# The last row tile's probabilities of pairs 5 to 16: 32x32 transposes in place by VectorE, blocks moved by ScalarE and GpSimd

## The chip, the core and the metric

The kernel runs on one core of a Trainium2 chip. The metric is the device time of one execution in microseconds (us), taken over several runs. Five engines work side by side: TensorE (PE in the profile; its weight loads are a row of their own, PEld), VectorE (DVE), ScalarE (ACT), GpSimd (POOL) and SyncE (SP), which issues all DMAs here. Each runs its own instructions strictly in the order in which the program lists them, and waits on semaphores for the others.

## The reference

Attention with a causal mask and a bias from a running sum, then two mixture layers on the result (shapes: 4 batches, 8 heads, 576 positions, head size 64):

```python
scores = scale * np.matmul(q, k.transpose(0, 1, 3, 2))
cum = np.cumsum(np.maximum(s, 0.0), axis=-1)
bias = -(cum[:, :, :, None] - cum[:, :, None, :])
scores = np.where(causal, -1000000000.0, scores + np.minimum(bias, 0.0))
attn = np.exp(scores - np.max(scores, axis=-1, keepdims=True))
attn = attn / (np.sum(attn, axis=-1, keepdims=True) + 1e-09)
x = np.matmul(attn, v)                                     # then (2304, 512)
x = np.maximum(np.maximum(x @ w1, x @ w2), x @ w3) @ w_out # d_ff 768
h = x @ w_in                                               # d_ff 2048
g = (a[0] + a[1]*h + a[2]*h**2 + a[3]*h**3) / (1.0 + abs(b[0])*abs(h) + abs(b[1])*h**2 + 1e-6)
out = g @ w_out2
```

## The kernel before

**Pairs.** The 32 heads go in 16 pairs (`pr` 0 to 15 in the code; pairs 1 to 16 in the title). The two heads of a pair (`y` 0 and 1) lie in the two halves of the partitions. For each pair the scores are made in five row tiles of queries, `i` 0 to 4: 64 rows, then four times 128. Causality cuts the keys, so tile `i` holds 64 + 128 `i` keys per head, and the last one, tile 4, is 128 queries by 576 keys.

**One pair, step by step.** `scores` makes the products on TensorE in four groups of two PSUM banks; VectorE adds the mask, takes the row minimum of the negated scores and writes the tile `P[i]` in SBUF (one buffer each); ScalarE takes the exponential in place and sums the rows; `norm` divides by the sum, on GpSimd or ScalarE. `flip` then turns each 128x128 block of `P` with keys on the free axis into one with keys on the partitions: a TensorE transpose against `ident` into a PSUM bank, and a copy of the bank (by ScalarE or VectorE) into the SBUF tile `PT`. There are six flip groups a pair, listed in `TBK`: tiles 2, 1, both heads of tile 4 apart, and both heads of tile 3 apart. 64-wide end blocks of both heads are flipped together ("lone" blocks, line 540; the others are line 545) and land in `PTC`. `values` multiplies the flipped probabilities by V on TensorE (line 597, two heads side by side in the array) into a group of 320 and one of 256 queries, and the result is split into a high and a low part, the tile `x` of the pair.

**What surrounds it.** Four pairs make one batch. The products of the first mixture layer for a batch (`experts`, line 187, 128x288) are issued among the attention steps of the next batch, 12 to a result; the last batch has its own stretch after the last pair. The second mixture layer (lines 187 and 944, 384 and 512 columns) fills the rest. Its weights and those of the first layer are loaded as raw words (`raww`), decoded by three VectorE steps (lines 639, 642, 644) and, for the second layer, written to DRAM (`w2_dram`, 36 "spills") and read back into `ws` tiles, once the SBUF of attention is given up.

**The order.** A planner (`Plan.issue`) sets the order on every engine when the program is built: each step has a rank, a cost written into the code for each engine that may take it, and what it reads and writes. A step that may run on several engines (`anyof`) goes where the cost, weighted by a price per engine, is least at that moment. A DMA's end is reckoned from a wire rate. On the chip only the order remains; the costs play no part.

Of the kernel before, what the change touches and what calls it, by code (L numbers as in the profile page):

```python
# [8 lines left out]
F32 = mybir.dt.float32  # L9
# [15 lines left out]
class Plan:  # L25
# [38 lines left out]
    def issue(self):  # L64
# [71 lines left out]
def kernel(  # L136
# [92 lines left out]
    PR = lambda pr: None if pr > 3 else {"dve": 1.0, "act": 1.0, "pool": 0.8}  # L229
# [37 lines left out]
    mask = at.tile([128, S + 128], F32, name="mask")  # L267
# [8 lines left out]
    P = [at.tile([128, 2 * (r0 + nr)], F32, name=f"P{i}") for i, (r0, nr) in enumerate(IT)]  # L276
# [73 lines left out]
    def consts():  # L350
        nc.gpsimd.memset(mask, 0.0)
        for at0, n, base in ((S, 128, 0), (0, 64, -64), (64, 64, 0)):
            nc.gpsimd.affine_select(
                out=mask[:, at0:at0 + n], in_=mask[:, at0:at0 + n], compare_op=ALU.is_ge,
                fill=-BIG / scale, base=base, pattern=[[-1, n]], channel_multiplier=1)

# [36 lines left out]
    plan.add({"pool": 1.2}, 0.1, lambda: pads(1), (), [("vh", 1, y) for y in range(2)], pre=e_dma)  # L393

# [46 lines left out]
    SB = [[(2, 0, 320, 0), (1, 0, 192, 320)], [(0, 0, 64, 0), (4, 0, 320, 64)], [(4, 320, S, 0)], [(3, 0, 448, 0)]]  # L441

    TBK = [((2, (0, 1)), ()), ((1, (0, 1)), (1, 2, 0)), ((4, (0,)), ()), ((4, (1,)), ()), ((3, (0,)), ()), ((3, (1,)), (3, 4))]
# [6 lines left out]
    def scores(pr, gs, rank):  # L450
# [3 lines left out]
        u = pr % 2  # L454
        Q, K, E = QK["q"][u], QK["k"][u], EXT[u]
        holds = {g: [Hold(), Hold()] for g in gs}
        sm = smalls[u]
        ops = [(Q[:, 0], K[:, 0]), (Q[:, 0], K[:, 1]), (Q[:, 1], K[:, 0]), (E[:, 1], E[:, 0])]

        def mms():  # L460
            for g in gs:
                for i, j0, j1, at0 in SB[g]:
                    r0, nr = IT[i]
                    b1, nb = 2 * i - j0 // 64, (j1 - j0) // 64
                    for x, (l, r) in enumerate(ops):
                        for y in range(2):
                            h = slice(64 * y, 64 * y + 64)
                            keys = r[h, j0:j1]
                            if y and i:
# [7 lines left out]
        for g, i, j0, j1, at0 in [(g, *x) for g in gs for x in SB[g]]:  # L477
# [4 lines left out]
            for y in range(2):  # L482
                m0 = S if i == 0 else j0 if y else S + 128 - W + j0
                m = smc(y, i)
                Pi = P[i][:, y * W:y * W + W]
                part = 3 if (i == 4 and j0 == 0) else 0
                ve(rank + 0.02, j1 - j0, lambda y=y, i=i, j0=j0, j1=j1, at0=at0, m=m, Pi=Pi, part=part, nr=nr, m0=m0, hold=hold:
                   nc.vector.tensor_tensor_reduce(  # L488
                       Pi[0:nr, j0:j1], hold[y].bank[0:nr, at0:at0 + j1 - j0], mask[0:nr, m0:m0 + j1 - j0], -scale,
                       sm[0:nr, 3, m:m + 1] if (i == 4 and j0 > 0) else 3.0e38, ALU.add, ALU.min, sm[0:nr, part, m:m + 1]),  # L490
                   [("sb", pr, g), ("s turn", g % 2), "const"] + ([("m3", pr, y)] if j0 > 0 else []),
                   [("P", y, i)] + ([("m3", pr, y)] if part else [("mn", pr, y, i)]), free=[hold[y]] if last else (),
                   cost=c_dve(j1 - j0))
                if j1 == W:
                    ac(rank + 0.04, 0, lambda Pi=Pi, W=W, m=m, nr=nr: nc.scalar.activation(  # L495
                        out=Pi[0:nr, 0:W], in_=Pi[0:nr, 0:W], func=ACTF.Exp,
# [9 lines left out]
    def norm(pr, tiles, rank):  # L506
# [10 lines left out]
        for i in tiles:  # L517
            for y in range(2):
                r0, nr = IT[i]
                t = P[i][0:nr, y * (r0 + nr):(y + 1) * (r0 + nr)]  # L520
                m = smc(y, i)
# [6 lines left out]

    def flip(pr, g, rank):
        hold = Hold()  # L530
        (i, ys), lone = TBK[g]
        n = 128 * i * len(ys)

        def tr():


            for x in ((), (), (1, 0), (1, 0, 2))[len(lone)]:
# [9 lines left out]
        def ev(e):  # L547
# [11 lines left out]
            if lone:  # L559
# [7 lines left out]
              [("tb", pr, g), ("t turn", t_turn(pr, g))], [("PT", g)], [hold], e_dma if pr == 0 else (), PR(pr))  # L567
# [14 lines left out]
    def values(pr, gis, rank):  # L582
# [8 lines left out]
        work = [[x for x in w if x[2] < x[3]] for w in work]  # L591

        def mms():
            for gi, b0, b1, hold in parts:
                for lone, j, q0, q1 in work[gi]:
                    for y in range(2):
                        nc.tensor.matmul(  # L597
                            hold.bank[64 * y:64 * y + 64, q0 - b0:q1 - b0], VH[u][:, j, y] if lone else V[u][y][:, j],
                            PTC[:, 64 * LONE[j]:64 * LONE[j] + 64] if lone else PTT[:, PH * y + SKEW * j + q0 - 64:PH * y + SKEW * j + q1 - 64],
# [3 lines left out]
        gs = [g for g in range(6) if (1 if g > 1 else 0) in gis]  # L603
        pe(rank, sum(0.01 + 4 * (q1 - q0) / 2400.0 for gi in gis for _, _, q0, q1 in work[gi]), mms,
# [415 lines left out]
```

## Time and profile before

| | |
|---|---|
| median of 3 runs | 889.09 us (888.07 to 890.43) |
| the profiled execution | 888.37 us |
| its span, first to last instruction | 886.6 us (1.8 us lie around it) |
| TensorE busy | 874.3 us, 99% of the span |
| VectorE, ScalarE, GpSimd busy | 663.2, 503.1, 341.0 us |
| granted TensorE clock, mean | 0.998 |

Busy times are sums of the instructions' spans. A matmul's span covers its way through the array, while the next one has already begun, so the busy share of TensorE does not tell how fast one follows another; the chain of work and the starts of instructions do.

### The profile page before, as it was taken

The numbers are of one execution on the slowest core, as the hardware profiler recorded it, in microseconds if no ns is written. First come the engines' busy times: TensorE is split into PE (matmuls) and PEld (weight loads), VectorE is DVE, ScalarE is ACT, GpSimd is POOL, SyncE is SP. The second block draws the span as 40 slices with busy tenths as digits, with TensorE's granted clock in tenths as the row PEclk, the third lists the DMA queues.
The fourth block names the chain that finished last, engine by engine and source line by source line (L and its number), as shares of the span: only waits on it lengthen the run. The fifth ranks groups of instructions, "written<-read, shape, count | busy, mean of one in ns | idle before, by whom it ended". The sixth has DMA issues, their size and how long they took to land.

```text
span 886.6 us, 17346 instructions
## 1 busy us (share of the span) xinstructions
PE 874.3 (99%) x6278; PEld 808.6 (91%) x6278; DVE 663.2 (75%) x1471; ACT 503.1 (57%) x1183; POOL 341.0 (38%) x404
## 2 busy tenths in 40 slices
PE   8889999999999999999999999999999999999998
PEld 7778998999999999999999989999999999999997
DVE  8999788868668775676896688488658747874875
ACT  7887455647545541222864666376557637653764
POOL 4467654423322320000873454254335315531432
PEclk9999999999999999999999999999999999999999
DMA  6798766577665565764100110020001001000100
GB/s 167 183 217 199 212 189 206 166 220 197 192 197 179 182 194 178 269 214 127 64 1 0 51 39 1 27 63 1 1 28 63 0 28 63 1 1 1 37 1 35
DMA packets 80662, 92.99 MB, mean 105 GB/s; under 512 B 33792, under 2 KB 61952, under 8 KB 80544
## 3 DMA queue, kind: packets, MB, share of 16 engines
q1 hardware_dynamic: 80576, 91.89, 35.4%
q8 instruction: 49, 0.80, 0.4%
q14 instruction: 37, 0.30, 0.1%
HBM read 69.96 MB, written 21.82 MB: 104 GB/s over the span
## 4 chain that ended last, share of the span: by engine, by line
PE 92%; DVE 4%; DMA 2%; POOL 1%; issue 1%; ACT 1%; SPq 0%; DVEq 0%; POOLq 0%; ACTq 0%
PE bank L187 56%; PE bank L944 23%; PE bank L471 4%; PE bank L597 4%; PE bank L545 3%; DVE P L488 1%; PE bank L540 1%; DMA raw_q<-in_q_dram 1%; DMA v<-in_v_dram 1%; SPq L245 0%; DVE wx L644 0%; DVE bank L639 0%; DVE T_q L432 0%; DMA EXT<-PT 0%; PE bank L417 0%
## 5 line engine op out<-in xcount | busy, mean ns | idle before, releaser
L187 PE MATMUL bank<-x,w 128*128 128x288 f32 x1728 | 243.3, 297 | 0.0
L187 PEld LDWEIGHTS bank<-x,w 128*128 128x128 f32 x1728 | 231.0, 188 | 4.6 <-issue 2.1
L944 PE MATMUL bank<-ws,g 128*128 128x512 f32 x864 | 215.4, 393 | 0.0
L187 PE MATMUL bank<-x,ws 128*128 128x384 f32 x1008 | 190.2, 336 | 0.0
L944 PEld LDWEIGHTS bank<-ws,g 128*128 128x128 f32 x864 | 160.8, 188 | 29.4 <-DVE g L924 0.2
L187 PEld LDWEIGHTS bank<-x,ws 128*128 128x128 f32 x1008 | 178.2, 188 | 7.1
L900 POOL TENSOR_SCALAR q<-a,cf 128x384 f32<-128x384 f32 x96 | 63.6, 662 | 183.6 <-ACT a L895 181.4
L495 ACT ACTIVATE P<-P,small 128x320 f32<-128x320 f32 (+4 forms) x160 | 88.4, 556 | 30.1 <-DVE small L488 30.0
L902 POOL TENSOR_TENSOR q<-q,a 128x384 f32<-128x384 f32 x96 | 97.7, 1018 | 8.0
L917 DVE SCALAR_TENSOR_TENSOR q<-q,cf,bank 128x384 f32<-128x384 f32 x96 | 58.8, 613 | 55.2 <-ACT bank L915 53.4
L723 DVE TENSOR_TENSOR hs<-bank,hs 128x288 f32<-128x288 f32 x96 | 43.6, 454 | 66.7 <-PE bank L187 64.7
L504 POOL TENSOR_SCALAR P<-P,small 128x320 f32<-128x320 f32 (+4 forms) x80 | 51.8, 662 | 108.1 <-DVE small L514 64.5
L242 POOL TENSOR_TENSOR h<-h 128x384 fp32r<-128x384 f32 x30 | 32.2, 1081 | 149.4 <-ACT h L811 135.1
L912 ACT ACTIVATE a<-q,cf 128x384 f32<-128x384 f32 x96 | 59.2, 617 | 39.4 <-POOL q L902 39.1
L187 PE MATMUL bank<-h,ws 128*128 128x384 f32 x432 | 75.9, 336 | 0.0
L923 ACT CAST g<-t 128x384 fp32r<-128x384 f32 x96 | 49.4, 514 | 46.5 <-DVE t L921 46.1
L187 PEld LDWEIGHTS bank<-h,ws 128*128 128x128 f32 x432 | 75.0, 188 | 0.5
L895 ACT ACTIVATE a<-bank 128x384 f32<-128x384 f32 x96 | 46.8, 487 | 35.8 <-PE bank L187 35.6
L239 ACT COPY hs<-bank 128x288 f32<-128x288 f32 x46 | 18.2, 396 | 82.2 <-PE bank L187 79.4
L488 DVE CUSTOM_DVE_ANT_0 P<-bank,mask 128x320 f32<-128x320 f32 (+3 forms) x160 | 61.0, 427 | 4.7 <-PE bank L471 3.3
L897 ACT ACTIVATE t<-bank,cf 128x384 f32<-128x384 f32 x96 | 64.0, 666 | 0.3 <-DVE g L924 0.3
L903 DVE TENSOR_TENSOR t<-bank,t 128x384 f32<-128x384 f32 x96 | 52.9, 551 | 14.7 <-ACT t L897 14.7
(102 smaller groups left out, 1282.6 us busy)
## 6 DMA issues: line engine op xcount, KB each, us to landing
raww<-in_moe_w_out_dram SPq DMA_DIRECT2D x22, 512.0 KB
raww<-in_moe_w_dram SPq DMA_DIRECT2D x18, 512.0 KB
w_dram<-wx SPq DMA_DIRECT2D x36, 256.0 KB
ws<-w_dram SPq DMA_DIRECT2D x36, 256.0 KB
raw_k<-in_k_dram SPq DMA_DIRECT2D x52, 140.0 KB
raw_q<-in_q_dram SPq DMA_DIRECT2D x52, 140.0 KB
raww<-in_moe_w_in_dram SPq DMA_DIRECT2D x14, 512.0 KB
h_dram<-hs SPq DMA_DIRECT2D x48, 144.0 KB
```

The costliest lines, as they stand in the source:

```text
L187: nc.tensor.matmul(ps, l, r, start=begin and i == 0, stop=end and i == len(seq) - 1)
L488: nc.vector.tensor_tensor_reduce(Pi[0:nr, j0:j1], hold[y].bank[0:nr, at0:at0 + j1 - j0], mask[0:nr, m0:m0 + j1 - j0], -scale, sm[0:nr, 3, ...
L495: ac(rank + 0.04, 0, lambda Pi=Pi, W=W, m=m, nr=nr: nc.scalar.activation(out=Pi[0:nr, 0:W], in_=Pi[0:nr, 0:W], func=ACTF.Exp, bias=sm[0:nr ...
L504: (nc.vector if e == "dve" else nc.gpsimd).tensor_scalar(t, t, c, 0.0, ALU.mult, ALU.add)
L897: ac(rank, 0, lambda: nc.scalar.activation(out=t2[kt], in_=hold.bank[:, 0:TB], func=ACTF.Identity, scale=cf[:, 3:4], bias=cf[:, 2:3]), [(" ...
L900: po(rank, 0, lambda: nc.gpsimd.tensor_scalar(t2[kq], t2[ka], cf[:, 5:6], cf[:, 4:5], ALU.mult, ALU.add), [ka, "cf4"], [kq], cost=0.75)
L902: po(rank, 0, lambda: nc.gpsimd.tensor_tensor(t2[kq], t2[kq], t2[ka], ALU.mult), [ka], [kq], cost=0.97)
L903: ve(rank, TB, lambda: nc.vector.tensor_tensor(t2[kt], hold.bank[:, 0:TB], t2[kt], ALU.mult), [("hp", ci)], [kt])
L912: ac(rank, 0, lambda: nc.scalar.activation(out=t2[a], in_=t2[qq], func=ACTF.Ln, bias=cf[:, 6:7], scale=1.0), [kq, "cf6"], [ka], cost=0.52)
L917: ve(rank, 0, lambda: nc.vector.scalar_tensor_tensor(t2[qq], t2[qq], cf[:, 6:7], hold.bank[:, 0:TB], ALU.add, ALU.mult), [kr], [kq], cost= ...
L923: ac(rank, TB, lambda: nc.scalar.copy(out=t2[kg][:, 0, :], in_=t2[t]), [kt], [kg], cost=0.41)
L944: nc.tensor.matmul(hold.bank, t2[kg][:, ga, ts], w2["o2", fc][:, wb, :], start=(fc == 0 and x == 0), stop=(fc == KF2 - 1 and x == 2))
```

## The change

For pairs 5 to 16 (`DV`, `pr` 4 to 15) tile 4 does not go through `flip` any more. Its keys are taken in another column order by the score matmuls (`parts_of`), so that each head fills blocks of 160 columns in a tile `P[4]` of 1280 columns, viewed as `P4` (4 parts, 2 heads, 160). Two parts of each head have 32 unused columns, which GpSimd fills first (`gaps`). VectorE transposes 32x32 blocks in place, one instruction of 640 columns a head (`regroup`), and 16 copies of 32 partitions by 320 columns, each by ScalarE or GpSimd, carry the blocks to their partitions in `PT` (view `PTB`). `values` reads queries 448 to 575 from there, so the products over queries 320 to 575 are cut at 448. The score groups and the two normalising steps are put in another order for these pairs (`SBS`, `NORM`), two flip groups fall away (`TBKS`), the mask gets extra columns (`mask4`), and flips and copies at the border between the two layouts wait for the values of the pair before. Three numbers of the planner differ too: the wire rate (225 after 70 us of plan instead of 190), the ranks of the spills (7 to 17 instead of 7 to 15) and of the first weights (half a pair later).

```diff
-                wire = max(wire, start + cost) + kb / 190.0
+                wire = max(wire, start + cost) + kb / (190.0 if wire < 70.0 else 225.0)
...
+    P = [at.tile([128, 2 * (r0 + nr) if i < 4 else 1280], F32, name=f"P{i}") for i, (r0, nr) in enumerate(IT)]
+    DV = set(range(4, NP))
+    P4 = P[4].rearrange("p (g y f) -> p g y f", g=4, y=2)
...
+    PTB = PTT[:, 1792:3072].rearrange("p (a y m c) -> p m y a c", a=4, y=2, m=5)
...
+    NORM = [(2, 1, 0), (4, 3)], [(4, 1, 0), (2, 3)]
...
+    SBS = ([[(2, 0, 320, 0), (1, 0, 192, 320)], [(0, 0, 64, 0), (4, 0, 320, 64)], [(4, 320, S, 0)], [(3, 0, 448, 0)]],
+           [[(4, 0, 320, 0), (1, 0, 192, 320)], [(0, 0, 64, 0), (4, 320, S, 64)], [(2, 0, 320, 0)], [(3, 0, 448, 0)]])
+    TBKS = ([((2, (0, 1)), ()), ((1, (0, 1)), (1, 2, 0)), ((4, (0,)), ()), ((4, (1,)), ()), ((3, (0,)), ()), ((3, (1,)), (3, 4))],
+            [((2, (0, 1)), ()), ((1, (0, 1)), (1, 2, 0)), ((3, (0,)), ()), ((3, (1,)), (3,))])
...
+    def gaps(pr, rank):
+        def fill():
+            for y in range(2):
+                nc.gpsimd.memset(P4[:, 2 - 2 * y:4 - 2 * y, y, 128:160], BIG)
+        po(rank, 0, fill, (), [("P", y, 4) for y in range(2)], cost=0.3)
+
+    def regroup(pr, rank):
+        for y in range(2):
+            ve(rank, 0, lambda y=y: nc.vector.transpose(out=P4[:, :, y], in_=P4[:, :, y]), (), [("P", y, 4)], cost=0.83)
+        for a in range(4):
+            for g in range(4):
+                anyof({"act": 0.42, "pool": 0.5}, rank + 0.05, lambda e, a=a, g=g: copy(
+                    e, PTT[32 * g:32 * g + 32, 1792 + 320 * a:2112 + 320 * a], P[4][32 * a:32 * a + 32, 320 * g:320 * g + 320]),
+                      [("P", y, 4) for y in range(2)], [("PT", 8 + 4 * a + g)], (), val[pr - 1] if pr - 1 not in DV else ())
...
+            work[1] = [x for lone, j, q0, q1 in work[1] for x in ((lone, j, q0, min(q1, 448)), (lone, j, max(q0, 448), q1)) if x[2] < x[3]]
...
+                return PTB[:, j, y, 2:] if lone else PTB[:, j, y]
...
-    S0, S1 = 7.0, 15.0
+    S0, S1 = 7.0, 17.0
...
-            rank = m_rank(0, 6 * fc) - 1.6
+            rank = m_rank(0, 6 * fc) - 1.1
...
+        if pr in DV:
+            gaps(pr, pr - 0.2)
...
+        if pr in DV:
+            regroup(pr, pr + 0.3)
+        for g in range(len(TBKS[pr in DV])):
```

What the planner makes of it shows in the order of the instructions. First TensorE, among the products of batch 2: the flips of one pair, where `P_100` is tile 4, `P_99` tile 3, `P_98` tile 2, `P_97` tile 1, and line 187 the first of twelve expert products. Before:

```order
L545 MATMUL bank_69<-ident,P_100 128x128 x4
L545 MATMUL bank_68<-ident,P_100 128x128 x4
L187 MATMUL bank_72<-x_318,w_1_0_132 128x288
...
L545 MATMUL bank_66<-ident,P_99 128x128 x3
L540 MATMUL bank_70<-ident,P_100 128x128
L540 MATMUL bank_70<-ident,P_99 128x128
L545 MATMUL bank_70<-ident,P_99 128x128 x3
```

And of the changed kernel (lines 610 and 605 are the former 545 and 540):

```order
L610 MATMUL bank_67<-ident,P_97 128x128 x2
L187 MATMUL bank_68<-x_318,w_2_0_135 128x288
...
L610 MATMUL bank_66<-ident,P_99 128x128 x3
L605 MATMUL bank_69<-ident,P_99 128x128
L610 MATMUL bank_69<-ident,P_99 128x128 x3
```

The two runs of four on tile 4 and the lone block of tile 4 are gone, nine transposes; the flips of tiles 2 and 1 now stand directly ahead of those of tile 3, with one group of twelve expert products between.

Then VectorE, at the place where tile 4 of one pair is treated. `wx` is a weight in decoding, `hs` an expert result, `small` the row minima and sums. Before:

```order
L639 TENSOR_SCALAR wx_111<-raww_109 128x512
L513 TENSOR_SCALAR small_102<-small_102 128x6
L514 RECIPROCAL small_102<-small_102 128x6
L642 SCALAR_TENSOR_TENSOR wx_111<-raww_109,wx_111 128x512
L488 ISA P_100,small_102<-bank_66,mask,small_102 128x256
L488 ISA small_102 128x1
L644 SCALAR_TENSOR_TENSOR wx_111<-raww_109,wx_111 128x512
```

And of the changed kernel (decoding is lines 713, 716 and 718 there, experts line 797):

```order
L718 SCALAR_TENSOR_TENSOR wx_112<-raww_110,wx_112 128x512
L585 STREAM_TRANSPOSE P_100<-P_100 128x4x160 x2
L797 TENSOR_TENSOR hs_121<-bank_71,hs_121 128x288
L713 TENSOR_SCALAR wx_111<-raww_109 128x512
L797 TENSOR_TENSOR hs_121<-bank_72,hs_121 128x288
L716 SCALAR_TENSOR_TENSOR wx_111<-raww_109,wx_111 128x512
L529 ISA P_99,small_103<-bank_66,mask 128x448
```

The two transposes are new, and stand ahead of the expert results that empty PSUM banks (`bank_71`, `bank_72`) and of the reduction of tile 3.

## Rows read from the trace of the kernel before

**Rows 1.** The page's first part: busy us, share, instructions.

```profile
PE 874.3 (99%) x6278; PEld 808.6 (91%) x6278; DVE 663.2 (75%) x1471; ACT 503.1 (57%) x1183; POOL 341.0 (38%) x404
```

**Rows 2.** Busy us by engine in stretches; then granted clock, DMA share, GB/s.

```profile
40.00:60.00 20.00, 17.09 (x179) 14.70 (x178) 19.81 (x66) 15.74 (x48) 13.49 (x17) 0.91 1.04 231
60.00:80.00 20.00, 19.36 (x198) 16.29 (x198) 19.04 (x56) 16.98 (x54) 15.41 (x17) 1.00 0.79 206
160.00:180.00 20.00, 20.00 (x200) 17.99 (x199) 19.14 (x50) 12.46 (x39) 8.85 (x10) 1.00 0.65 196
80.00:345.00 265.00, 264.24 (x2479) 247.27 (x2476) 200.70 (x536) 141.20 (x407) 92.72 (x108) 1.00 0.66 194
345.00:432.00 87.00, 87.00 (x614) 87.00 (x613) 60.44 (x119) 24.72 (x54) 9.94 (x12) 1.00 0.57 187
```

**Rows 3.** The chain that ended last, 206 to 223 us: start, us, what.

```profile
206.72 1.81 PE bank L187 x12
208.52 0.44 PE bank L545 x4
208.96 0.33 PE bank L540 x3
209.29 0.22 PE bank L545 x2
209.51 1.60 PE bank L187 x12
...
223.01 2.90 PE bank L597 x44
```

**Rows 4.** TensorE's timeline, value products of one pair: start, us, instruction, shape.

```profile
223.10 0.60 PE L597 MATMUL bank<-PT,v 128*64 128x256 f32 x4
223.54 0.28 PE L597 MATMUL bank<-PT,vh 128*64 128x64 f32 x4
223.65 0.39 PE L597 MATMUL bank<-PT,v 128*64 128x128 f32 x4
223.87 0.28 PE L597 MATMUL bank<-PT,vh 128*64 128x64 f32 x4
```

**Rows 5.** Line 545: ns minimum/median/maximum of one transpose, first and last start.

```profile
L545 PE MATMUL bank<-ident,P x320: 270/273/421, 16.7 to 335.3; 128*128 128x128 f32 x160
```

**Rows 6.** VectorE lines 432, 642, 644: ns minimum/median/maximum of one.

```profile
L432 DVE STREAM_TRANSPOSE T_q<-raw_q x13: 1239/1250/1264, 28.2 to 287.0; 128x576 f32<-128x576 f32 x13
...
L642 DVE SCALAR_TENSOR_TENSOR wx<-raww,wx x48: 649/693/1554, 72.4 to 352.3; 128x512 uint32<-128x512 uint32 x48
...
L644 DVE SCALAR_TENSOR_TENSOR wx<-raww,wx x48: 650/691/1800, 73.5 to 353.0; 128x512 uint32<-128x512 uint32 x48
```

**Rows 7.** Line groups, 72 to 345 us: busy us, mean ns, idle before.

```profile
L642 DVE SCALAR_TENSOR_TENSOR wx<-raww,wx 128x512 uint32<-128x512 uint32 x46 | 36.5, 793 | 1.0
L644 DVE SCALAR_TENSOR_TENSOR wx<-raww,wx 128x512 uint32<-128x512 uint32 x46 | 34.7, 754 | 0.6
...
L239 ACT COPY PT<-bank 128x512 f32<-128x512 f32 x35 | 19.1, 581 | 5.2 <-PE bank L545 5.1
...
L495 ACT ACTIVATE P<-P,small 128x320 f32<-128x320 f32 x22 | 12.3, 560 | 12.0 <-DVE small L488 12.0
...
L504 POOL TENSOR_SCALAR P<-P,small 128x320 f32<-128x320 f32 x16 | 11.3, 714 | 82.1 <-DVE small L514 45.7 <-PE bank L187 27.2 <-ACT hs L239 5.5
```

**Rows 8.** Timeline at 166 us: a decode step beside a GpSimd instruction.

```profile
165.77 1.87 POOL L242 TENSOR_TENSOR qkT<-T_q,qkT 128x576 fp32r<-128x576 f32 x1
166.39 1.80 DVE L644 SCALAR_TENSOR_TENSOR wx<-raww,wx 128x512 uint32<-128x512 uint32 x1
```

**Rows 9.** SyncE's timeline: the last spill, then the first weights back.

```profile
353.70 0.32 SPq L245 DMA_DIRECT2D w_dram<-wx  x1
354.07 3.29 SPq L245 DMA_DIRECT2D ws<-w_dram  x7
```

**Rows 10.** What TensorE waited for, 80 to 345 us: total us, times, longest.

```profile
PE bank L545 <- ACT P L502: 0.7, 1, 0.7
```

More of the change, by code (lines that the diff above doesn't have):

```diff
@@ L355, in consts, with mask4 @@
                 fill=-BIG / scale, base=base, pattern=[[-1, n]], channel_multiplier=1)
+    def mask4():
+        nc.gpsimd.memset(MASK4[0], 0.0)
+        nc.gpsimd.memset(mask[:, S + 128:S + 256], 0.0)
+        for t, base in ((mask[:, S + 224:S + 256], -32), (MASK4[0][:, 0, 128:], -64), (MASK4[0][:, 1, 128:], -96)):
+            nc.gpsimd.affine_select(out=t, in_=t, compare_op=ALU.is_ge, fill=-BIG / scale, base=base, pattern=[[-1, 32]],
+                                    channel_multiplier=1)
     def pads(u):
@@ L488, in scores, with src @@
+                def src(y=y, j0=j0, j1=j1, at0=at0, nr=nr, hold=hold, split=dv and i == 4):
+                    t = hold[y].bank[0:nr, at0:at0 + j1 - j0]
+                    return t.rearrange("p (g f) -> p g f", g=2) if split else t
+                ve(rank + 0.02, j1 - j0, lambda i=i, j0=j0, m=m, dst=dst, bias=bias, part=part, nr=nr, src=src:
                    nc.vector.tensor_tensor_reduce(
-                       Pi[0:nr, j0:j1], hold[y].bank[0:nr, at0:at0 + j1 - j0], mask[0:nr, m0:m0 + j1 - j0], -scale,
+                       dst, src(), bias, -scale,
@@ L490, in scores @@
                        sm[0:nr, 3, m:m + 1] if (i == 4 and j0 > 0) else 3.0e38, ALU.add, ALU.min, sm[0:nr, part, m:m + 1]),
-                   [("sb", pr, g), ("s turn", g % 2), "const"] + ([("m3", pr, y)] if j0 > 0 else []),
-                   [("P", y, i)] + ([("m3", pr, y)] if part else [("mn", pr, y, i)]), free=[hold[y]] if last else (),
+                   [("sb", pr, g), ("s turn", g % 2), "mask4" if dv else "const"] + ([("sbx", pr, g, y)] if last else []) + ([("m3", pr, y)] if j0 > 0 else []),
@@ L493, in scores @@
+                   [("P", y, i)] + ([("m3", pr, y)] if part else [("mn", pr, y, i)]) + ([] if last else [("sbx", pr, g, y)]), free=[hold[y]] if last else (),
                    cost=c_dve(j1 - j0))
                 if j1 == W:
-                    ac(rank + 0.04, 0, lambda Pi=Pi, W=W, m=m, nr=nr: nc.scalar.activation(
-                        out=Pi[0:nr, 0:W], in_=Pi[0:nr, 0:W], func=ACTF.Exp,
+                    Pi = Pi if dv and i == 4 else Pi[0:nr, 0:W]
+                    ac(rank + 0.04, 0, lambda Pi=Pi, m=m, nr=nr: nc.scalar.activation(
+                        out=Pi, in_=Pi, func=ACTF.Exp,
@@ L534, in tr @@
         def tr():
-            for x in ((), (), (1, 0), (1, 0, 2))[len(lone)]:
+            for x in ((), (0,), (1, 0), (1, 0, 2))[len(lone)]:
                 l = lone[x]
```

60 lines of the change are left out of this document (40 added, 20 removed).

## The prediction

> **What bounds the kernel now.** I read the page's busy shares first: TensorE is busy 99% of the span, VectorE 75%, ScalarE 57%, GpSimd 38% [rows 1]. Such spans overlap, so I asked next for the busy times stage by stage. From 80 to 345 us, where the attention of pairs 5 to 16 runs between expert products, TensorE is busy 264.24 of 265 us, and then 87.00 of 87 until the last batch is through [rows 2]. The waits of that stage confirm it: one wait of 0.7 us in TensorE's own row [rows 10]. There the time is the sum of what stands in TensorE's queue, and an instruction taken from the queue is time gained, as long as the others keep up. The others come next. VectorE is busy 200.70 of 265 us (76%), ScalarE 141.20 (53%), GpSimd 92.72 (35%). Ahead of 80 us it is otherwise: from 40 to 60 us VectorE is busy 19.81 of 20 us and TensorE loses 2.91, with a mean granted clock of 0.91; from 60 to 80 VectorE has 19.04 and TensorE loses 0.64. But a VectorE at 19.14 of 20 costs TensorE nothing from 160 to 180 [rows 2], where expert products stand between the attention steps.
>
> **What is removed.** Nine transposes a pair (eight blocks of tile 4 and its lone block), in 12 pairs: 108. The duration of one is 273 ns [rows 5], but they overlap. In the chain four take 0.44 us, three 0.33 and two 0.22, so each adds 0.110 us, and the nine of that run last from 208.52 to 209.51 [rows 3]. 108 x 0.110 = 11.9 us. With them 24 copies of 512 columns leave ScalarE (31 become 7 in the program's order).
>
> **What is added on TensorE.** The three products of 256 columns over the later queries become six of 128, for each head. Four records of 256 columns take 0.44 us from start to start (223.10 to 223.54), of 128 columns 0.22 (223.65 to 223.87), of 64 columns 0.11 [rows 4]: time follows columns, and the columns stay 44 records in 2.90 us [rows 3] worth. Nothing, then, up to the reading precision of some 0.02 us for each of 36 further groups, 0.7 us; I take 0.2. The moving operand is now gathered from runs of 32 columns; no row has that, and I put no price on it beyond this 0.7. Twelve expert products behind a score group take 1.81 us, behind a transpose 1.60 [rows 3], so a turn between split and whole use of the array costs 0.2 us. Counted in the two orders there are 92 such turns before and 93 now: 0.2 us.
>
> **What is added on VectorE.** 24 transposes of 640 columns. The same operation on 576 columns takes 1250 ns [rows 6], but writes with a step of 18 elements; scaled to 640 this gives 1.39 us, the upper bound. A two-input step of 512 columns takes at least 650 ns [rows 6], scaled 0.81, the lower one. The new transposes write whole runs of 32, so I take 1.1 us between the two: 26 us (19 to 33).
>
> **What is added on ScalarE and GpSimd.** 87 of the 192 copies stand in ScalarE's queue, 105 in GpSimd's. For ScalarE the bounds of one are 0.36 us (the bank copy of 512 columns, 581 ns, scaled) and 0.56 (an exponential of 320 columns); for GpSimd 0.36 likewise and 0.71 (a scaling of 320 columns) [rows 7]. With 0.46 and 0.6 that is 40 and 63 us. ScalarE gets 24 x 0.58 = 14 us back and comes to (141 + 26) / 254 = 66%, GpSimd to (93 + 63) / 254 = 61%, where 254 is the 265 us less some 11. The 24 fills fit into the rest. Neither becomes the bound by its sum.
>
> **Contention.** Decoding steps on VectorE are stretched where GpSimd works: a step with a median of 691 ns takes 1.80 us beside a GpSimd instruction of 1.87 us [rows 6, 8]. On the mean the two steps are (793 - 693) + (754 - 691) = 163 ns above their medians [rows 6, 7], at a GpSimd share of 35%. At 61% I take this in proportion: 163 x 61/35 = 284 ns, 0.12 us more for each of 46 weights, 6 us. VectorE then comes to (200.7 + 26 + 6) / 254 = 92%; with the bounds 86% to 94%.
> The Trainium skill has a harder rule for this place ("SBUF — State Buffer", section "Who interferes with whom"): a VectorE instruction with two SBUF inputs contends with a GpSimd instruction that reads SBUF, and whoever comes first holds the shared ports for the whole instruction. The 1.80 us agree with it. Taken to its end (each of the 92 two-input steps meets a copy and waits for half of it, 0.36 us) it would add 33 us instead of 6, and VectorE would stand at 102%; that is the slower rival below. I stay with the mean excess, because the trace has all meetings in it, at the share of GpSimd that it has.
>
> **What TensorE loses by it.** Rows at such a VectorE load are 60 to 80 us (95%, TensorE loses 3.2%) and 160 to 180 us (96%, nothing) [rows 2]. The changed stage has expert products among its steps like the second. I take 1% of 254 us, 2.5 us (0 to 8.1).
> New waits are part of this. The value products now wait for 16 copies behind both transposes, and `P[4]`, one buffer, is written for the next pair only when these are out. On GpSimd the two fills of the next pair wait for ScalarE's copies, with weight splits and scalings of `P` queued behind. Between the value products of two pairs stand some 17 us of score groups, expert products and flips; 8 copies of 0.5 us on each engine lie under them. Without that cover they would cost up to 4 us a pair.
>
> **The planner's numbers.** No instruction goes with them; they shift loads. SyncE's order is the same up to its 40th row; then the fourth weight load steps behind a pair's q and k. The spills end later in rank. In the trace the first return of weights follows the last spill at 354.07 us [rows 9], 78 us ahead of the end of the last batch's products, and TensorE waits for none. Counted in stores of expert results, the first return stands behind the 34th of 48 in the new order and the 36th in the old, so the cover stays. I take nothing for both.
>
> **The sum.** Against the profiled execution: 888.4 - 11.9 + 0.2 + 0.2 + 2.5 = 879.4 us. That execution lies 0.7 us under the median of the runs shown, so I predict 880 us as a median.
>
> **The rivals.**
> *VectorE late, most of the gain eaten.* The whole stage loses 3.2% as from 60 to 80 us: 8.1 us in place of 2.5, 885 us. For it: the 92%, and two transposes standing ahead of the steps that free banks. Against it: 160 to 180 us.
> *VectorE the bound, slower.* Transposes at 1.39 us and steps blocked by copies bring its load to that of 40 to 60 us, 99%, where TensorE loses 14.6% [rows 2]. If half of the stage does so, 0.146 x 127 = 18.5 us are lost: 888.4 - 11.5 + 18.5 = 895 us. It decides from a loss of 11.5 / 254 = 4.5%. For it: the 1.80 us. Against it: before 80 us there are few expert products to fill in, later there are many.
> *The gain does not arrive.* TensorE passes the stage sooner and waits for returning weights instead, since spills reach further: 888 to 889 us. Against it: the 78 us of cover.
> *Transposes cost their full duration.* If each removed one freed 273 ns [rows 5], 108 of them would give 29.5 us, 859 us. The chain speaks against it [rows 3].
> The Trainium skill ("TensorE: Matmul & The Clock Gate", Part 4) has some 275 ns for a transpose in a kernel's context; the span agrees, the distance of starts does not.
>
> **How the numbers follow.** Forecast 0.69, gain mostly eaten 0.13, VectorE the bound 0.10, no arrival 0.06, full duration 0.02. The forecast's own range is 875.5 to 885: below, no loss at all (877 on the median's scale) and 1.5 us for seams that fall away with the runs; above, the loss bound less what the likelier half excludes. The range to 888 takes in the second case and part of the third; left out are the slower rival, the full duration and some edge, under 2 in 10. Faster by over 0.3% (2.7 us, about what a measurement of this kernel can tell) is under 886.4: 0.69 + 0.11 + 0.02 = 0.82. Within it: 0.02 + 0.06 = 0.08. Slower: 0.10.
>
> **What would show it.** Nine fewer transposes a pair, the rest still 0.110 us apart; the value products of a pair still at 2.9 us; expert products at 1.6 us a dozen; the stage from 80 us on shorter by 9 us, the stretch after it unchanged. The transposes of 640 columns at 0.8 to 1.4 us and VectorE near 92% there. I am wrong if TensorE waits over 8 us in that stage, for the copies (line 238) or for VectorE's reductions, or if the value products take over 3.1 us a pair.

## The result and the profile after

The changed kernel takes 895.55 us in the median of 6 runs (892.69 to 897.2), against 889.08 (888.07 to 890.43) for the kernel before: a ratio of 1.0070 [1.0054, 1.0086]. It is slower by 6.5 us, where I had forecast 9 us less. The profiled execution took 896.71 us.

The page's first part, of the changed kernel:

```profile
span 894.9 us, 17664 instructions
...
PE 870.1 (97%) x6314; PEld 808.4 (90%) x6314; DVE 684.6 (76%) x1494; ACT 537.5 (60%) x1255; POOL 402.9 (45%) x530
```

TensorE is busy 4.2 us less than before [rows 1], and the span is 8.3 us longer, so TensorE stands still 24.8 us (894.9 - 870.1) where it stood 12.3 (886.6 - 874.3). That is one half of the story. The other half is in the stretches (each line: from and to in us, length, then the busy time of PE, PEld, DVE, ACT and POOL, granted clock, DMA share, GB/s):

```profile
40.00:60.00 20.00, 18.74 (x197) 15.48 (x193) 19.82 (x64) 16.88 (x50) 14.30 (x19) 0.91 0.88 210
60.00:80.00 20.00, 18.16 (x174) 15.77 (x175) 19.73 (x53) 16.68 (x46) 11.52 (x21) 1.00 0.66 170
80.00:140.00 60.00, 55.41 (x557) 51.38 (x555) 59.55 (x140) 42.36 (x120) 48.00 (x59) 1.00 0.73 195
140.00:160.00 20.00, 15.14 (x116) 14.52 (x118) 17.44 (x43) 12.47 (x36) 12.91 (x17) 0.83 0.66 190
80.00:345.00 265.00, 251.70 (x2452) 238.79 (x2451) 231.55 (x581) 171.52 (x483) 155.51 (x225) 0.99 0.71 202
345.00:432.00 87.00, 87.00 (x662) 86.62 (x661) 49.67 (x99) 22.45 (x52) 9.20 (x9) 1.00 0.56 169
```

Against [rows 2]: from 80 to 345 us TensorE lost 0.76 us and now loses 13.3, which is as much as its idle time grew in all. Over the whole stage VectorE is at 87% and GpSimd at 59%, near my estimates; but from 80 to 140 us VectorE is at 99% (59.55 of 60), so the mean hid the place (that a full VectorE is not the cause by itself, the experiments show). And from 140 to 160 us the granted clock is 0.83, a part of that time at the lower of TensorE's two levels (1.2 in place of 2.4 GHz).

What TensorE waited for in the whole execution (us, times, longest):

```profile
PE bank L610 <- POOL P L546: 11.2, 5, 4.9
PE bank L671 <- DMA v<-in_v_dram: 2.3, 1, 2.3
...
PE bank L502 <- ACT PT L238: 0.8, 1, 0.8
```

The wait that counts is none of those I had named. TensorE's transposes (line 610) wait for GpSimd's scalings of `P` (line 546), in five waits; copies (line 238) have 0.8 us. The longest ended at 148.62 us. TensorE's timeline there (start, us, instruction; in brackets the idle time ahead and what ended it), and one later pair's flips:

```profile
141.91 1.85 PE L187 MATMUL bank<-x,w 128*128 128x288 f32 x12
148.62 1.12 PE L610 MATMUL bank<-ident,P 128*128 128x128 f32 x4 [4.86 <-POOL P L546]
...
150.46 3.23 PE L187 MATMUL bank<-x,w 128*128 128x288 f32 x12
...
225.06 0.60 PE L610 MATMUL bank<-ident,P 128*128 128x128 f32 x4
225.49 0.49 PE L605 MATMUL bank<-ident,P 128*128 128x128 f32 x3
```

GpSimd's timeline up to the same point:

```profile
140.73 4.78 POOL L238 COPY PT<-P 32x320 f32<-32x320 f32 x7
145.57 0.61 POOL L238 CAST w<-wx 128x512 fp32r<-128x512 f32 x1
146.26 1.59 POOL L241 TENSOR_TENSOR w<-wx,w 128x512 fp32r<-128x512 f32 x1
147.83 1.34 POOL L546 TENSOR_SCALAR P<-P,small 128x320 f32<-128x320 f32 x2
```

And VectorE's, whose `small` steps (lines 555 and 556) give the factors of that scaling:

```profile
142.76 0.88 DVE L718 SCALAR_TENSOR_TENSOR wx<-raww,wx 128x512 uint32<-128x512 uint32 x1
143.56 0.67 DVE L713 TENSOR_SCALAR wx<-raww 128x512 uint32<-128x512 uint32 x1
144.16 0.44 DVE L797 TENSOR_TENSOR hs<-bank,hs 128x288 f32<-128x288 f32 x1
144.52 0.67 DVE L716 SCALAR_TENSOR_TENSOR wx<-raww,wx 128x512 uint32<-128x512 uint32 x1
145.12 0.42 DVE L555 TENSOR_SCALAR small<-small 128x4 f32<-128x4 f32 x1
145.57 0.18 DVE L556 RECIPROCAL small<-small 128x4 f32<-128x4 f32 x1
```

`small` needs the row sums, and the last of them is read on ScalarE by 144.03:

```profile
143.84 0.19 ACT L537 ACTIVATION_READ_ACCUMULATOR P<-P,small 128x1 f32 x1
```

`small` starts at 145.12, behind an expert addition and a decode step. Its factors are there at 145.75, and the seven copies are out at 145.5; but next in GpSimd's queue stands the split of a weight (`w`), 2.3 us, and only then, at 147.83, the two scalings. TensorE has run out of expert products at 143.76 and stands. Then the dozen of expert products that took 1.85 us takes 3.23, at the lower clock. So this stall is paid twice. The second longest wait, 2.98 us, ended at 265.14 and is of another mixture: the row sums were read only at 263.16, the factors were there at 263.74 and eleven copies out of GpSimd's queue at 264.01, so there the copies made the smaller part.

The sum by parts, from the profiled executions: idle time +12.5 us. The clock: a mean of 0.992 over 894.9 us is short of full by 7.2 us, 0.998 over 886.6 by 1.8, so +5.4. The work that went: -11.9. The forecast's two small terms on TensorE: +0.4. Together +6.4, of +8.3 in the span; the rest I can't assign. The clock's part is the weakest of these. Runs of the kernel before whose times lie within 0.3 us of each other have mean clocks from 0.997 to 1.000, which is 2.7 us; and TensorE stood still in some of the slow time. Nor is all of it behind the stall: 3.4 of the 5.4 us are from 140 to 160 us (0.83 over 20 us), and 1.8 from 20 to 40 us, ahead of the first transpose of 640 columns at 70.9 us. Before, then after:

```profile
20.00:40.00 20.00, 18.11 (x213) 14.95 (x211) 18.96 (x66) 17.72 (x59) 7.87 (x12) 1.00 0.72 164
20.00:40.00 20.00, 17.43 (x191) 14.37 (x188) 16.23 (x59) 15.79 (x53) 6.70 (x9) 0.91 0.75 171
```

The kernel with the planner's numbers alone (first run below) has 0.91 there as well.

The costs of the added work, in line groups of the changed kernel, 72 to 345 us (busy us, mean ns, idle before):

```profile
L238 POOL COPY PT<-P 32x320 f32<-32x320 f32 x105 | 58.6, 558 | 13.7 <-DVE P L585 8.5 <-DVE hs L797 0.9
...
L238 ACT COPY PT<-P 32x320 f32<-32x320 f32 x87 | 39.8, 457 | 11.5 <-DVE P L585 10.3
L716 DVE SCALAR_TENSOR_TENSOR wx<-raww,wx 128x512 uint32<-128x512 uint32 x48 | 39.4, 821 | 0.8
L718 DVE SCALAR_TENSOR_TENSOR wx<-raww,wx 128x512 uint32<-128x512 uint32 x48 | 39.1, 814 | 0.7
...
L585 DVE STREAM_TRANSPOSE P<-P 128x640 f32<-128x640 f32 x23 | 18.6, 830 | 1.6 <-ACT P L544 1.6
```

### The profile page after: what moved, and what is told of

Its sections match the earlier page's. It is cut to its first block, busy times and chain, and to the rows that moved or that the text cites. A ratio compares the mean times of both kernels' runs of the same rounds, so it can differ in the third digit from the quotient of the medians.

```text
span 894.9 us, 17664 instructions
## 1 busy us (share of the span) xinstructions
PE 870.1 (97%) x6314; PEld 808.4 (90%) x6314; DVE 684.6 (76%) x1494; ACT 537.5 (60%) x1255; POOL 402.9 (45%) x530
## 4 chain that ended last, share of the span: by engine, by line
PE 80%; DVE 8%; POOL 6%; DMA 3%; issue 2%; SPq 1%; ACT 1%; DVEq 0%; POOLq 0%
PE bank L187 50%; PE bank L1022 22%; PE bank L671 3%; POOL PT L238 3%; PE bank L502 2%; PE bank L610 2%; DVE P L529 2%; DVE wx L718 1%; POOL P L546 1%; DVE wx L716 1%; SPq L244 1%; DVE T_q L453 1%; DVE P L585 1%; DMA ext_dram<-PT 1%; PE bank L605 1%
## 5 line engine op out<-in xcount | busy, mean ns | idle before, releaser
L978 POOL TENSOR_SCALAR q<-a,cf 128x384 f32<-128x384 f32 x96 | 65.8, 686 | 181.9 <-ACT a L973 181.6
L537 ACT ACTIVATE P<-P,small 128x192 f32<-128x192 f32 (+5 forms) x160 | 89.8, 565 | 28.8 <-DVE small L529 28.3
L546 POOL TENSOR_SCALAR P<-P,small 128x320 f32<-128x320 f32 (+5 forms) x80 | 54.3, 692 | 93.3 <-DVE small L556 50.3
L238 POOL COPY PT<-P 32x320 f32<-32x320 f32 x105 | 58.6, 558 | 13.7 <-DVE P L585 8.5
L982 DVE SCALAR_TENSOR_TENSOR t<-t,cf,bank 128x384 f32<-128x384 f32 x96 | 58.8, 613 | 2.4
```

The source lines that it names most:

```text
L238: nc.scalar.copy(out=out, in_=in_) if e == "act" else (nc.vector if e == "dve" else nc.gpsimd).tensor_copy(out, in_)
L537: ac(rank + 0.04, 0, lambda Pi=Pi, m=m, nr=nr: nc.scalar.activation(out=Pi, in_=Pi, func=ACTF.Exp, bias=sm[0:nr, 0, m:m + 1], scale=-1.0, ...
L546: (nc.vector if e == "dve" else nc.gpsimd).tensor_scalar(t, t, c, 0.0, ALU.mult, ALU.add)
L978: po(rank, 0, lambda: nc.gpsimd.tensor_scalar(t2[kq], t2[ka], cf[:, 5:6], cf[:, 4:5], ALU.mult, ALU.add), [ka, "cf4"], [kq], cost=0.75)
L982: ve(rank, 0, lambda: nc.vector.scalar_tensor_tensor(t2[kt], t2[kt], cf[:, 1:2], hold.bank[:, 0:TB], ALU.add, ALU.mult), [("hp", ci), ("h ...
```

## The experiments

My theory after the result was that GpSimd's queue makes TensorE wait (theory 1). The rivals: VectorE's load from 40 to 140 us (2), and the planner's numbers or the new order by themselves (3). Each ratio below is to the kernel before, run on the same chip (888.45 to 888.99 us).

**One part alone, or moved.** The first four runs take the change apart. The planner's numbers without the new way (the mask columns stay in):

```diff
-    DV = set(range(4, NP))
+    DV = set()
```

> The changed kernel with no pair treated in the new way (DV empty): only the planner's three numbers and the mask columns differ from the kernel before. If the planner's numbers make the loss, this run is slower than before by some 6 us (895 us). If GpSimd's queue does (copies ahead of the scalings that TensorE waits for, 11.2 us of such waits in the changed kernel), or VectorE's load between 40 and 140 us, it is within 3 us of 889, with at most 2 us of waits of TensorE for GpSimd's scalings.

Measured 893.36 us, 1.0051 [1.0036, 1.0066]. The numbers that I had priced at nothing cost 4.7 us in the old way. From 80 to 140 us this kernel has:

```profile
80.00:140.00 60.00, 57.75 (x530) 53.51 (x525) 52.58 (x121) 29.14 (x82) 32.84 (x36) 0.97 0.71 195
```

TensorE loses 2.25 us there and some clock, where it lost nothing before. Next the new way with the three old numbers:

```diff
-                wire = max(wire, start + cost) + kb / (190.0 if wire < 70.0 else 225.0)
+                wire = max(wire, start + cost) + kb / 190.0
...
-    S0, S1 = 7.0, 17.0
+    S0, S1 = 7.0, 15.0
...
-            rank = m_rank(0, 6 * fc) - 1.1
+            rank = m_rank(0, 6 * fc) - 1.6
```

> The changed kernel with the planner's numbers of the kernel before (wire 190, spills to 15, weights 1.6 ahead). If the numbers make the loss: 880 us, the gain of 11.9 us on TensorE less small stalls. If GpSimd's queue or VectorE's load does: 892 to 900 us, with waits of TensorE for GpSimd's scalings of 8 us or more.

Measured 895.14 us, 1.0075 [1.0060, 1.0090]: no better. So the loss is not the numbers' alone. All 192 copies on ScalarE:

```diff
-                anyof({"act": 0.42, "pool": 0.5}, rank + 0.05, lambda e, a=a, g=g: copy(
+                anyof({"act": 0.42}, rank + 0.05, lambda e, a=a, g=g: copy(
```

> The changed kernel with all 192 copies on ScalarE, none on GpSimd. If GpSimd's queue makes the loss, TensorE's waits for GpSimd's scalings fall from 11.2 to under 3 us, and the time to 882 to 887 us, unless ScalarE's 16 copies of 0.46 us a pair take the place. If it is VectorE's load by the transposes alone, 893 us or more with VectorE still over 19.5 of 20 us from 40 to 140 us. If the copies on GpSimd only stretched VectorE's decoding steps, their means fall from 0.82 us to 0.78 or less and VectorE's load with them.

Measured 898.17 us, 1.0107 [1.0090, 1.0124], the slowest of all. TensorE's waits mostly change their name:

```profile
PE bank L187 <- DVE hs L238: 5.4, 6, 2.1
PE bank L610 <- POOL P L546: 4.1, 3, 2.5
PE bank L610 <- ACT PT L238: 3.9, 1, 3.9
```

From 80 to 140 us VectorE has some room here (56.34 of 60 us), and yet TensorE loses 8.9 us, where the changed kernel lost 4.6:

```profile
80.00:140.00 60.00, 51.13 (x493) 47.16 (x494) 56.34 (x131) 45.99 (x126) 45.86 (x52) 0.91 0.72 196
```

The new way for pairs 9 to 16 alone, with the new numbers:

```diff
-    DV = set(range(4, NP))
+    DV = set(range(8, NP))
```

> The changed kernel with the new way from pair 9 on (8 pairs in place of 12), so that the stretch in which the first layer's weights are decoded (to about 140 us) is left as before. If VectorE's load in that stretch makes the loss: 8 x 0.99 = 7.9 us gained on TensorE, 882 us. If GpSimd's queue does wherever the copies stand: 886 to 892 us, with waits of 2 us or more for GpSimd's scalings after 180 us.

Measured 892.02 us, 1.0034 [1.0021, 1.0048]. Of its 7.4 us of waits for line 546, 3.7 came after 180 us.

**Parts left out in a fixed order.** Here the planner's costs are as they were, so the order stays, and only the instruction is not issued. First the gain by itself: the kernel before, without tile 4's transposes of pairs 5 to 16.

```diff
                 l = lone[x]
+                if l == 4 and pr > 3:
+                    continue
...
                 for j in range(i):
+                    if i == 4 and pr > 3:
+                        continue
```

> The kernel before, in its own order, without the nine transposes of tile 4 in pairs 5 to 16 (108 in all); their bank copies stay, so tile 4's probabilities are left out of the later values and stale bank contents stand there. Nothing is added anywhere. If a removed transpose frees its 0.110 us on TensorE, 888.7 - 11.9 = 877 us (876 to 879). If it frees its whole span of 273 ns, 859 us. If TensorE then waits for what was hidden under the transposes (bank copies, reductions), 882 us or more, with TensorE's idle time up from 12 us.

Measured 876.89 us (876.82 to 877.13), 0.9859 [0.9843, 0.9876]: 11.9 us less, the term of my sum to the tenth. The span is 875.2 us and the clock 1.000. Then the changed kernel without GpSimd's copies, without ScalarE's, and without VectorE's transposes:

```diff
-                anyof({"act": 0.42, "pool": 0.5}, rank + 0.05, lambda e, a=a, g=g: copy(
+                anyof({"act": 0.42, "pool": 0.5}, rank + 0.05, lambda e, a=a, g=g: (e == "pool" and pr > 4) or copy(
...
-                anyof({"act": 0.42, "pool": 0.5}, rank + 0.05, lambda e, a=a, g=g: copy(
+                anyof({"act": 0.42, "pool": 0.5}, rank + 0.05, lambda e, a=a, g=g: (e == "act" and pr > 4) or copy(
...
-            ve(rank, 0, lambda y=y: nc.vector.transpose(out=P4[:, :, y], in_=P4[:, :, y]), (), [("P", y, 4)], cost=0.83)
+            ve(rank, 0, lambda y=y: None, (), [("P", y, 4)], cost=0.83)
```

> The changed kernel in its own order, without the copies of tile 4's blocks that stand in GpSimd's queue, from the second of the twelve pairs on (so parts of the probabilities are left out of the values); all else as it was. Theory 1 (scalings of P wait in GpSimd's queue behind the copies): TensorE's waits for line 546 fall from 21 us to under 6, the clock loss behind them goes, and the time is 880 to 885 us. Theory 2 (VectorE, at 99% from 40 to 140 us, is late): the waits move to VectorE or stay, 891 to 895 us, no more gained than GpSimd's smaller use of shared memory gives VectorE. Theory 3 (the planner's new order itself, whatever the copies cost): 890 us or more.

> The changed kernel in its own order, without the copies of tile 4's blocks that stand in ScalarE's queue, from the second of the twelve pairs on (parts of the probabilities are left out of the values). Theory 1: the stalls for GpSimd's scalings stay, 893 to 896 us. Theory 2: the same, 893 to 896. Theory 3: 893 to 896. If ScalarE's copies were the hidden cause, under 889 us.

> The changed kernel in its own order, without the 24 transposes of 640 columns on VectorE (tile 4's blocks stay unturned), which took 0.83 us each, 20 us in all. Theory 1 (GpSimd's queue): the copies start some 1.7 us earlier behind the scalings, the stalls for line 546 shrink little, 892 to 895 us. Theory 2 (VectorE's load): VectorE falls below 95% from 80 to 140 us, TensorE's idle time there falls by more than half, 882 to 887 us. Theory 3 (order): 890 us or more, with the stalls at the same places.

Measured: without GpSimd's copies 888.26 us (886.57 to 891.54), 0.9991 [0.9978, 1.0005]; without ScalarE's 893.07, 1.0036 [1.0020, 1.0052]; without VectorE's transposes 888.24 (885.28 to 889.66), 0.9991 [0.9978, 1.0003]. Leaving out GpSimd's copies or VectorE's transposes gives 7.3 us each, ScalarE's copies 2.5. Neither theory 1 (880 to 885 without GpSimd's copies) nor theory 2 (882 to 887 without the transposes, and nothing without the copies) is right alone. The longest stall shows why, in TensorE's timeline. Without GpSimd's copies:

```profile
144.16 0.66 PE L610 MATMUL bank<-ident,P 128*128 128x128 f32 x4 [2.64 <-POOL P L546]
```

Without VectorE's transposes:

```profile
145.53 1.11 PE L610 MATMUL bank<-ident,P 128*128 128x128 f32 x4 [3.51 <-POOL P L546]
```

Without ScalarE's copies:

```profile
148.02 1.03 PE L610 MATMUL bank<-ident,P 128*128 128x128 f32 x4 [4.87 <-POOL P L546]
```

4.86 us became 2.64, 3.51 and 4.87: copies on GpSimd and transposes on VectorE stand in one chain ahead of the same scaling, ScalarE's copies do not. Waits for line 546 fell from 11.2 us (not 21, as the expectation has it) to 4.3 without GpSimd's copies and to 6.2 without the transposes. The stretches, without GpSimd's copies:

```profile
80.00:140.00 60.00, 57.45 (x581) 52.38 (x580) 59.59 (x143) 43.85 (x121) 38.07 (x42) 1.00 0.75 203
80.00:345.00 265.00, 258.84 (x2541) 244.72 (x2540) 226.13 (x580) 173.24 (x483) 103.52 (x128) 0.99 0.71 204
```

Without VectorE's transposes:

```profile
80.00:140.00 60.00, 55.79 (x579) 52.03 (x577) 57.25 (x135) 43.20 (x119) 49.70 (x60) 1.00 0.75 201
80.00:345.00 265.00, 257.28 (x2540) 244.60 (x2539) 215.49 (x555) 172.69 (x481) 154.49 (x222) 0.99 0.71 204
```

TensorE's idle time of 13.3 us falls to 6.2 and 7.7. Without the copies VectorE is as full as before from 80 to 140 us (59.59 of 60), and TensorE loses 2.6 us there in place of 4.6; without the transposes VectorE has more room (57.25), and TensorE still loses 4.2. So VectorE's share in that stretch, the measure of theory 2, does not tell what TensorE loses. All three cuts together (those lines combined):

> The changed kernel in its own order, without any of the 16 copies a pair (from the second of the twelve pairs on) and without the 24 transposes on VectorE; the blocks of tile 4 are left out of the later values. Without GpSimd's copies alone, and without the transposes alone, the changed kernel lost 7 us each, without ScalarE's copies 2.5. If these add up, 895.6 - 7.3 - 7.3 - 2.5 = 878.5 us: the added work is the whole loss, and the order and the planner's numbers cost nothing by themselves. If all three were parts of one chain (VectorE late, then the copies, then the scalings), it stays near 886 us. If the order itself costs what the numbers alone cost in the kernel before (4.7 us), 877 + 4.7 = 881.5 us.

Measured 884.12 us, 0.9949 [0.9934, 0.9964]: 11.4 us less than the changed kernel, not the 17.1 of the parts added. They overlap. And 7.2 us over the 876.9 stay although only the copies of the first of the twelve pairs are left. VectorE is still full from 80 to 140 us, with none of the new transposes in it:

```profile
80.00:140.00 60.00, 57.17 (x585) 53.33 (x582) 59.46 (x138) 34.63 (x98) 40.78 (x46) 1.00 0.78 213
```

The same with the old numbers:

> The changed kernel with the planner's three numbers as before, without any of the 16 copies a pair (from the second of the twelve pairs on) and without the 24 transposes on VectorE; the blocks of tile 4 are left out of the later values. With the new numbers the same cut gave 884.1 us, against 877 for the transposes alone taken from the order before. If the numbers make the difference, 877 to 880 us; if the order of the changed steps and the new waits do, 882 to 886 us.

Measured 884.65 us, 0.9949 [0.9931, 0.9968]. These 7 us are not the numbers; they come with the new order of steps, the fills and the new waits, which these runs do not tell apart. Idle time is the smaller part of them: with the new numbers the profiled execution has a span of 880.8 us and TensorE stands still 15.6, against 13.6 of 875.2 in the kernel that only leaves out the transposes.

**Repairs.** First the planner's costs set to what the profile shows:

```diff
-anyof({"act": 0.42, "pool": 0.5}, rank + 0.05
+anyof({"act": 0.46, "pool": 0.68}, rank + 0.05
...
-    plan.add({"dve": 0.6 if bank else 0.4}
+    plan.add({"dve": 0.6}
...
-cost=0.5 if bank else 0.65)
+cost=0.5 if bank else 0.82)
...
-{"pool": 1.25, "dve": 0.68}
+{"pool": 1.5, "dve": 0.68}
```

> The change, planned with durations as the profile shows them: a copy 0.46 on ScalarE and 0.68 on GpSimd (0.42 and 0.5 in the change), decoding steps 0.6, 0.82, 0.82 (0.4, 0.65, 0.65), GpSimd's weight differences 1.5 (1.25). Theory A (the planner fits weight work into gaps that the chip does not have, so row sums and scalings come late): TensorE's waits for line 546 halve, 885 to 891 us. Theory B (there is simply too much work on VectorE and GpSimd from 40 to 140 us, in any order): 893 to 897 us.

Measured 888.21 us, 0.9994 [0.9985, 1.0004]; waits for line 546 fell from 11.2 to 4.0 us. The scalings of tiles 2 and 3 on ScalarE:

```diff
-                anyof({"pool": 0.35 + 0.00084 * n, "act": 0.2 + 0.00083 * n}, rank + 0.02,
+                anyof({"act": 0.2 + 0.00083 * n} if pr in DV and i in (2, 3) else {"pool": 0.35 + 0.00084 * n, "act": 0.2 + 0.00083 * n}, rank + 0.02,
```

> The change, with the scalings of tiles 2 and 3 in pairs 5 to 16 on ScalarE alone, so that the transposes of TensorE wait for no scaling in GpSimd's queue behind copies and weight splits; GpSimd gets 139 of the copies in return, ScalarE 53. If GpSimd's queue as such is the cause: waits for GpSimd's scalings fall from 11 us to under 3, 886 to 890 us. If VectorE's late sums (line 555) are as much the cause, ScalarE's scalings wait for them as well: 891 to 896 us, with TensorE's waits put down to line 544.

Measured 887.96 us, 0.9993 [0.9983, 1.0003]. Its waits:

```profile
PE bank L610 <- ACT P L544: 5.6, 5, 2.0
```

For GpSimd's scalings 0.2 us of waits are left, but half of the former 11.2 for ScalarE's: those also wait for `small`. The repairs take back 7.3 and 7.6 us, and neither gets clearly below the kernel before. A control, the kernel before with the same measured costs:

> The kernel before, planned with decoding steps at 0.6, 0.82, 0.82 and weight differences at 1.5, no other edit. If the measured costs repair what the change brought, the kernel before has nothing to gain: 887 to 891 us (and anything off 888.5 tells how far another order alone moves the time). If the costs were wrong for both, 884 us or less.

Measured 888.01 us, 0.9989 [0.9980, 0.9998]: there they are worth 0.4 us, so the 7.3 of the changed kernel are no gain that the old way would have had too. Both repairs, in all twelve pairs, with the new numbers and with the old:

> The change with its own three numbers, for all twelve pairs, with scalings of tiles 2 and 3 on ScalarE and the planner's costs as measured. If the old numbers spoiled the combined run (894.9 us): 883 to 886 us here. If the two repairs get in each other's way (ScalarE then has scalings and more of the copies, and TensorE waits for line 544): 888 to 895 us.

> The new way for all twelve pairs, with the old three numbers, scalings of tiles 2 and 3 on ScalarE and the planner's costs as measured. Each repair alone gave 888 us with the new numbers. If the repairs add up: 881 to 884 us. If VectorE's load from 40 to 140 us sets what is left: 886 to 889 us, no better than the new way in pairs 9 to 16.

Measured 891.09 us, 1.0023 [1.0013, 1.0033], and 894.85, 1.0059 [1.0043, 1.0075]. The repairs do not combine. The second one's waits:

```profile
PE bank L610 <- ACT P L544: 9.1, 6, 2.0
PE bank L610 <- ACT PT L238: 3.0, 2, 1.8
```

The scalings are late on ScalarE as they were on GpSimd, and again through more than one queue. Ahead of the longest wait, which ended at 309.30 us, two copies on ScalarE (from 306.42) hold up an exponential that the row sums need; in the one that ended at 148.11 the factors came from VectorE at 147.17, and the scaling started at 147.49. At last the new way behind the crowded stretch, in pairs 9 to 16, with the old numbers: by itself, with scalings on ScalarE, and with both repairs (edits as above).

> The new way for pairs 9 to 16 with the old three numbers, scalings wherever the planner puts them. If the numbers gave the 5.7 us between 892.0 and 886.3: 886 to 887 us. If the scalings on ScalarE gave it: 890 to 893 us, with waits of TensorE for line 546 above 6 us.

> The new way for pairs 9 to 16 only, that is behind the stretch in which VectorE is at 99%, with the planner's three numbers of the kernel before, and the scalings of tiles 2 and 3 of these pairs on ScalarE. 72 transposes fewer give 7.9 us at most: 881 us if nothing new is waited for. If the waits come with the new way wherever it stands, 888 us or more; if the numbers' 4.7 us in the changed kernel were separate from the rest, 887 us (892.0 of the run from pair 9 less 4.7).

> The new way for pairs 9 to 16, the old three numbers, scalings of tiles 2 and 3 of these pairs on ScalarE, and the planner's costs as measured (copies 0.46 and 0.68, decoding 0.6, 0.82, 0.82, weight differences 1.5). Without the measured costs this gave 886.3 us. If the two repairs are of separate waits: 882 to 884 us. If they mend the same wait (the scaling that TensorE waits for): 885 to 887 us. Waits of TensorE for lines 544 and 546 together were 6.4 us and cannot give more than that.

Measured 886.34 us, 0.9970 [0.9959, 0.9981]; 886.27, 0.9978 [0.9968, 0.9988]; 886.75, 0.9977 [0.9968, 0.9986]. All three beat both kernels, by some 2 us. It was the numbers that gave the 5.7 us between 892.02 and 886.34, not the scalings. In the first of the three, 80 to 140 us (pairs in the old way) is what it was before:

```profile
80.00:140.00 60.00, 60.00 (x573) 56.02 (x569) 50.84 (x125) 33.66 (x94) 36.65 (x40) 1.00 0.69 191
```

## Why the prediction was wrong

**What is removed: right.** 108 transposes at 0.110 us, 11.9 us; measured 11.9 by the run that only leaves them out. Four still take 0.43 us from start to start (225.06 to 225.49). The full duration of 273 ns is ruled out, which would have given 859 us.

**What is added on TensorE: right.** The value products of a pair took 2.91 us against 2.90 [rows 3], as the chain of the changed kernel has it:

```profile
206.65 2.91 PE bank L671 x56
```

The stretch after the attention did not change either: from the last pair's first value product to the end 546.3 us in both (886.6 - 340.26, 894.9 - 348.55). Those products, before and after:

```profile
340.26 0.34 PE L597 MATMUL bank<-PT 128*64 128x64 f32 x4
348.55 0.34 PE L671 MATMUL bank<-PT 128*64 128x64 f32 x4
```

**What is added elsewhere: sizes right, or too high.** A transpose of 640 columns took 0.83 us, at the lower end (0.81 to 1.39, taken 1.1). Copies took 0.457 and 0.558 (taken 0.46 and 0.6). Two decode steps stood 250 ns above their medians (821 - 693 + 814 - 692), against 284 taken; the size was near, but the reason given for it was not (last section). So VectorE came to 87%, not 92%, ScalarE to 65%, GpSimd to 59%.

**The step that failed** is "What TensorE loses by it": 2.5 us (0 to 8.1) taken from mean loads. It is 12.5 us of idle time, and the clock that fell behind a stall, some 3.4 us by its mean. "Neither becomes the bound by its sum" was true and did not matter. A scaling that TensorE needs stands in GpSimd's queue behind copies and a weight split, and its factors stand in VectorE's queue behind decode steps; I had named the scalings as queued work, and then priced only the copies' own cover. The runs without copies or transposes show that these cause most of it (7.3 us each, 11.4 with all cuts). That it is a chain through two queues, and not one full engine, is shown for the longest stall, which shrinks to 2.64 and 3.51 when either queue is relieved; for the other waits it is argued from this one. The Trainium skill ("PSUM — Partial Sum Buffer", section "Engine vs sequencer instructions") says that the queues of VectorE, ScalarE and GpSimd are strictly first in, first out; the scaling that waits 2.1 us for a weight split with its factors ready (145.75 to 147.83) agrees.

Where the loss lies can be summed, each run against the kernel before on its own chip: with the old numbers, pairs 9 to 16 alone bring -2.65 us (886.34 against 888.99) of the -7.9 that 72 transposes are worth, and all twelve pairs bring +6.49 (895.14 against 888.65), so pairs 5 to 8 add 9.1 instead of -4.0. So 13.1 of the 18.4 us lost belong to the four pairs that run between 60 and 160 us, where VectorE is busiest. It is not full there with the old numbers, though, from 80 to 140 us of that run:

```profile
80.00:140.00 60.00, 56.27 (x551) 52.26 (x549) 54.24 (x138) 46.03 (x128) 45.61 (x61) 0.94 0.64 179
```

**The second failed step** is "The planner's numbers ... I take nothing for both". I looked only at when weights return. They cost 4.7 us in the old way (with the mask columns) and 5.7 with the new way in pairs 9 to 16. In the changed kernel they make no difference that can be told (895.55 against 895.14); I suppose that the other loss covers them there. Which of the three does it was not tried.

**The rivals.** The time came out at that of "VectorE the bound, slower" (895 us), and a part of that rival was there: VectorE was full from 80 to 140 us and stayed without a gap until the longest stall was over, so 9.4 of the 13.3 us that TensorE lost (4.6 until 140 us, 4.9 until 160) fell beside a full VectorE; the other 3.8 came after 160 us with VectorE at 84%. But a transpose took 0.83 us, not 1.39, and a full VectorE was neither enough for the loss nor needed: with it as full, TensorE lost less without GpSimd's copies, and with it less full TensorE lost more with all copies on ScalarE. That the time agrees is luck. "The gain does not arrive", for weights that return late, is ruled out by the unchanged stretch after the attention. My signs of being wrong named waits over 8 us for copies or reductions; the size was right, but the waits were for scalings.

**Open:** the 7 us that the new order costs without the added work; and how much of any single repair is luck of the order, since the combined repairs came out 3 us worse than each alone, and 7 with the old numbers.

## What to carry to other kernels

Busy shares say whether an engine has time, not whether it is on time: for each instruction that the bounding engine waits for, read what stands ahead of it in its own queue and in the queues of its inputs, and price the added work there, in the most crowded stretch first. A stall of TensorE here cost idle time and then a half clock behind it. A new way can pay in one part of a kernel and cost in another; trying it on a part of the loop (here pairs 9 to 16) separates the two.

## What was not expected of the hardware

I had taken decode steps on VectorE to stretch in proportion to GpSimd's work. They did not. With GpSimd's copies left out (10 of 105 stay in this stretch) GpSimd is busy 103.52 of 265 us in place of 155.51, and the two steps still mean 839 and 792 ns against 821 and 814 with the copies; line groups, 72 to 345 us, of that run:

```profile
L716 DVE SCALAR_TENSOR_TENSOR wx<-raww,wx 128x512 uint32<-128x512 uint32 x48 | 40.3, 839 | 0.8
...
L718 DVE SCALAR_TENSOR_TENSOR wx<-raww,wx 128x512 uint32<-128x512 uint32 x48 | 38.0, 792 | 0.7
...
L238 POOL COPY PT<-P 32x320 f32<-32x320 f32 x10 | 5.0, 500 | 2.6 <-DVE P L585 2.2
```

Beside the run of seven copies a decode step took 0.88 us (142.76), some 0.19 over its median, not the 1.80 that one took beside a two-input instruction of GpSimd [rows 8]; the copies there took 0.68 each (4.78 / 7), against 0.558 on the mean. So the slower rival's case, in which each step waits for half a copy and takes 0.36 us more, did not come about: the two steps stand 0.13 and 0.12 us over their medians on the mean. What stretches the steps on the mean, if not the copies, no run here isolates.
